# A planner that prices the first half with measured times, a second accumulation bank for the first heads, and a margin on TensorE's operands

## The chip, the cores and the metric

The kernel runs on one core of one Trainium2 chip. The metric is the device time of one execution in microseconds (us), taken as the median of several runs. TensorE is called PE in the profile's rows, its weight loads PEld, VectorE DVE, ScalarE ACT, GpSimd POOL, and SyncE's DMA queue SP.

## The reference

Three layers follow each other: a causal attention with a bias, a dense layer with a gate, and eight experts whose weights come from a balanced gate.

```python
# attention: 4 batches, 8 heads, 576 positions, 64 wide
scores = scale * q @ k^T                    # causal
bias = -(cum[:, :, :, None] - cum[:, :, None, :]);  cum = cumsum(max(s, 0))
attn = softmax(where(causal, -1e9, scores + minimum(bias, 0)))
x = (attn @ v) as 2304 rows x 512
# first MoE (one dense expert, 512 -> 2048 -> 512)
h = x @ w_in;  x = (h * sigmoid(1.702 * h)) @ w_out
# second MoE (8 experts, 512 -> 1024 -> 512)
P = exp(x @ w_gate), 8 times normalised over rows and columns
out = sum_e P[:, e] * (relu(x @ w1[e]) @ w2[e])
```

## The kernel before

The program is written once, in the order of a planner that runs while the kernel is built. Class `Sequencer` keeps a model time for each engine (`free`), for each buffer what has touched it (`touched`), and lists of operations that are handed in but not yet placed (`held`). An operation that PE executes is placed at once. Those of the other engines are held, and `run` places them when PE's model time has reached the point at which they could start, first by rank, then by number. `cost` gives each operation its model duration; there are two sets of prices, a coarse one and a finer one that holds from the second MoE on (`fine`). So the planner's prices decide in what order the instructions of every engine stand in the program; on the chip each engine executes its list in that order.

What PE does next is chosen in the loop at the end of the first half: it asks the functions `can_vpow`, `can_flush`, `can_value`, `can_turn`, `can_score` and the first MoE's generator when their operands are settled in model time, and takes the first in this list that is ready. The steps are these:

- `scores` (written `sp` in rows): q times k for a block of queries into a bank `sp`. DVE reduces it against the mask (a custom instruction, `sm<-sp,mask`, called ISA where the order of a program is listed), ACT takes the exponential. The first 8 heads read `kf` in full 32 bit; later ones read two 32-bit-rounded parts, `one` and `two`, which ACT, DVE, POOL and a DMA prepare.
- `turn` (`tp`): PE transposes the exponentials; ACT or DVE copies them out (`pf` for the first 14 heads, `ph` and `pl` after).
- `values` (`op`): the weights times v, into one bank, tag "O", which `values` (line 856) allocates from the pool `ps_a`. `finish` then lets DVE divide (`stats<-op`, `xg<-op`), and the bank is free for the next head once that is done.
- `flush_x` (`xtp`): transposes a finished block of attention rows into `xh` and `xl`.
- the first MoE (`hp`, then `acc`): for a block of 256 rows (`j`) and a pair of 128 columns (`p`), 24 products of 128x256 into `hp` and 24 into `acc`. It needs the pair's weights `wih`, `wil`, `woh`, `wol`, which `conv` makes from 64-bit words: a load `st`, two ACT steps, a DVE step `t<-st`, a cast and a subtraction on DVE or POOL. There are 8 pairs, 4 chunks each; those of pairs 4 to 6 need memory that is only given free when the first 16 heads are nearly done (`convert`).

There are 64 half heads: `heads` alternates eight times 8 heads with 256 queries or 320 queries, in 128 units. In the program stand 192 reductions `sm<-sp`, and they are used below as marks: "the 16th reduction" stands after 16 others, in both programs behind the same score step. The marks used are the 16th (the first score of the ninth head), the 40th, the 48th and the 64th.

After the attention the first MoE does its last two blocks in a wide form (`accw`, 573 to 655 us), and the second MoE follows to the end.

Of the kernel before, what the change touches and what calls it, by code (L numbers as in the profile page):

```python
# [38 lines left out]
N_KF = 4  # L39
ADDING = 3.6  # L40
AFTER_OWN = 34
N_F = 14
NEXT_V = 11
LATE = 3000.0

LATENCY = {
# [3 lines left out]


class Op:
    __slots__ = ("engine", "call", "cost", "ready", "end", "waits", "after", "rank", "number", "nbytes", "late", "tail")


class Sequencer:
# [10 lines left out]
    def __init__(self):  # L67
        self.free = dict.fromkeys(self.ENGINES, 0.0)
        self.held = {e: [] for e in self.ENGINES}
        self.touched = {}  # L70
        self.earlier = {}
        self.rings = {}
        self.dma = self.issued = 0.0
        self.rank = 0
        self.holding = False
        self.fine = False
        self.late = 0.0
        self.count = 0
        self.outside = set()
# [13 lines left out]
    def settled(self, name, ap=None):  # L93

        t = 0.0
        for x in self.touched.get(name, ()):
            if ap is not None:
                _, cols = self.where(ap)
                if x[1][0] >= cols[1] or cols[0] >= x[1][1]:
                    continue  # L100
            if x[3].end is None:
                return float("inf")
            if x[3].engine != "PE":
                t = max(t, x[3].end + 200)
        return t

    @staticmethod
# [22 lines left out]
    def cost(self, engine, what, out, ins, sums=False):  # L130
        n = max(self.size(x) for x in [out] + ins[:2])
        psum = any(x.space == PSUM for x in ins)
        if self.fine:
            if engine == "PE":
                return self.size(out) * (4 if ins[0].dtype == F32 else 1) / 2.4 + (13 if ins[0].dtype == F32R else 2.7)
            by = any(self.size(x) == 1 for x in ins[1:]) and n > 1
            if engine == "DVE":
                quick = what in ("tensor_copy", "tensor_scalar") and not psum
                return 66 + 60 * by + n / (1.92 if quick else 0.96)
            if engine == "ACT":  # L140
                return (50 if psum else 90) + 100 * by + 93 * sums + n / 1.2
        if engine == "PE":
            n = self.size(out)
            if what == "transpose":
                return 2 * n / 2.4
            slow = ins[0].dtype == F32 or ins[0].dtype == F32R and n < 256
            return n * (4 if slow else 1) / 2.4
        if engine == "DVE":
            quick = what in ("tensor_copy", "tensor_scalar") and not psum
            return 70 + n / (1.92 if quick else 0.96)  # L150
        if engine == "ACT":
            return 90 + n / 1.2
        return 80 + n * {"memset": 0.3, "tensor_scalar": 2.7}.get(what, 2.24)


    def submit(self, engine, what, call, outs, ins, adds=False):
        op = Op()
        op.engine, op.call, op.end, op.rank, op.number = engine, call, None, self.rank, self.count
        op.ready, op.waits, op.after, op.nbytes, op.tail = 0.0, set(), [], 0, 0
        op.late = self.late + (2000 if self.fine and self.rank else 0)  # L160
        self.count += 1
        if what == "dma_start":
            op.cost = 60 if engine == "SP" else 1000
            op.nbytes = self.size(outs[0]) * outs[0].shape[0] * (2 if self.fine and outs[0].dtype == F16 else 4)
            if adds and self.fine:
                op.nbytes *= ADDING
        else:
            sums = len(outs) > 1
            op.cost = self.cost(engine, what, outs[0], ins, sums) + (190 if sums and not self.fine else 0)
            if self.fine:  # L170
                op.tail = {"DVE": 85, "ACT": 110}.get(engine, 0) + 90 * sums
        for ap, writes in [(x, False) for x in ins] + [(x, True) for x in outs]:
            name = ap.tensor.name
            if name in self.outside:
                continue
            parts, cols = self.where(ap)
            mine = self.touched.setdefault(name, [])
            for x in self.touched.get(self.earlier.get(name), ()):
                self.depend(op, x[3])
            for x in mine:  # L180
                if (writes or x[2]) and x[3] is not op and not (ap.space == DRAM and writes and x[2]):
                    if x[0][0] < parts[1] and parts[0] < x[0][1] and x[1][0] < cols[1] and cols[0] < x[1][1]:
                        self.depend(op, x[3])
            mine[:] = [
                x for x in mine
                if x[3].end is None or x[3].engine != engine or x[2] != writes or x[0] != parts or x[1] != cols
            ]
            mine.append((parts, cols, writes, op))
        if engine == "PE" or not self.holding:
            self.issue(op)  # L190
        else:
            self.held[engine].append(op)

    def depend(self, op, on):
        if on.end is None:
            op.waits.add(on)
            on.after.append(op)
        elif self.fine and on.engine == op.engine != "PE" and not on.nbytes:
            op.ready = max(op.ready, on.end + AFTER_OWN)
        elif on.engine != "PE" or op.engine != "PE":  # L200
            op.ready = max(op.ready, on.end + LATENCY.get((on.engine, op.engine), LATENCY.get(on.engine, 0)))

    def issue(self, op):
# [2 lines left out]
                self.issue(x)  # L206
        e = op.engine
        start = max(self.free[e], op.ready)
        self.free[e] = start + op.cost
        op.end = start + op.cost + op.tail  # L210
        if op.nbytes:
# [7 lines left out]
        for x in op.after:  # L219
            x.waits.discard(op)  # L220
            self.depend(x, op)
        op.after = None

    def when(self, op):

# [95 lines left out]
def kernel(  # L321
# [227 lines left out]
    begin = []  # L549
# [283 lines left out]
    def turn(i):  # L833
# [21 lines left out]
        )  # L855
        live[i] = (ph, pl, blocks, spots)

    def values(i):
        n, u = units[i]
        qb0 = extent(n)[6][0]  # L860
        v3 = v3_of[n]
        ph, pl, blocks, spots = live.pop(i)
        if u[0] == qb0:
            outs[n] = (
                ps_a.tile([128, 3, D + 1], F32, tag="O", name="op"), stats[:, 8 + n % 2 * 3:11 + n % 2 * 3]
            )
        op, den = outs[n]
        for m, (qb, rows, ke, a) in enumerate(blocks):
# [97 lines left out]
    def can_value():  # L966
# [3 lines left out]
        if n > n_fin:  # L970
            return never
        x = [live[n_v][0], live[n_v][1], *v3_of[n]]
        return max([seq.slot(ps_a, "O") if n not in outs else 0] + [seq.settled(a.tensor.name) for a in x])

    def do_value():
        nonlocal n_v
# [1017 lines left out]
    while moe1_can is not None:  # L1994
# [5 lines left out]
        more_scales()  # L2000
        seq.run()
        now = seq.free["PE"]
        times = [can_vpow(), can_flush(), can_value(), can_turn(), can_score(), moe1_can()]
        which = next((k for k, x in enumerate(times) if x <= now), None)
        if which is None:
            stuck += 1
            assert stuck < 3000
# [253 lines left out]
```

## Time and profile before

| | us |
|---|---|
| median of 3 runs | 1994.37 (1994.06 to 1995.16) |
| the profiled execution, its own time | 1995.91 |
| its span, first to last instruction | 1994.1 |
| PE busy | 1956.2 (98%) |
| DVE busy | 1427.6 (72%) |
| ACT busy | 1227.5 (62%) |
| POOL busy | 335.0 (17%) |

The page cuts the span in 40 slices and shows each engine's busy share. PE's busy time counts a matmul until its modelled end, so matmuls in a row overlap; the rate is read from start to start. The view of the windows gives, for any stretch, the busy time of each engine, the clock that TensorE was granted, and the share of time in which the DMA engines moved data. The timeline gives each instruction's start and duration, and in brackets the idle time of its engine just before it and what ended it.

### The profile page before, as it was taken

Reading aid. Unit: us, or ns where it says so; the run is one execution under the profiler, and the core shown is the slowest. Engines: PE = TensorE matmul, PEld = TensorE weight load, DVE = VectorE, ACT = ScalarE, POOL = GpSimd, SP = SyncE. Lnnn points to the kernel's source line nnn. Section 1 sums busy time; section 2 is a strip of 40 time slices with the busy share of each in tenths; the row PEclk is TensorE's granted clock in tenths of the full one; section 3 lists DMA queues with packets and bytes.
Section 4 is the critical chain, followed back from the end, with each engine's and each line's share of the span. In section 5 each row is a group of like instructions: output and inputs, shape, how many; then the busy total and the mean of one; then the engine's idle time right before and its main releaser. Section 6 shows DMA issues by size and latency. Waiting matters only on the chain.

```text
span 1994.1 us, 41095 instructions
## 1 busy us (share of the span) xinstructions
PE 1956.2 (98%) x15683; PEld 1575.5 (79%) x15683; DVE 1427.6 (72%) x3240; ACT 1227.5 (62%) x2525; POOL 335.0 (17%) x376
## 2 busy tenths in 40 slices
PE   6999999999999999999999999999999999999999
PEld 5889999999988677777777777777777777777777
DVE  5886776776743776887877767776787776776656
ACT  4776765766643665665666666656666666565343
POOL 3565444443300000000000011111100001111000
PEclk9999999999999999999999999999999999999999
DMA  7555444454335544565484565666648556566331
GB/s 221 159 178 181 138 131 138 129 146 116 86 94 186 208 152 146 202 232 182 147 273 133 153 186 156 172 197 184 167 120 261 147 150 186 156 172 183 119 130 43
DMA packets 230100, 322.11 MB, mean 162 GB/s; under 512 B 38272, under 2 KB 156224, under 8 KB 229904
## 3 DMA queue, kind: packets, MB, share of 16 engines
q1 hardware_dynamic: 216944, 295.90, 45.2%
q0 software_dynamic: 12960, 23.60, 8.2%
q8 instruction: 123, 2.02, 0.4%
q14 instruction: 73, 0.60, 0.1%
HBM read 230.85 MB, written 84.34 MB: 158 GB/s over the span
## 4 chain that ended last, share of the span: by engine, by line
PE 81%; DVE 9%; ACT 6%; DMA 2%; issue 1%; SPq 0%; POOL 0%; ACTq 0%; DVEq 0%
PE C L279 16%; PE A L279 16%; PE D L279 16%; PE hp L279 8%; PE B L279 8%; PE acc L279 5%; PE op L279 3%; PE sp L279 3%; PE tp L279 2%; ACT h L279 2%; PE accw L279 2%; DVE h L279 2%; DVE t L279 1%; DVE hst L279 1%; PE accx L279 1%
## 5 line engine op out<-in xcount | busy, mean ns | idle before, releaser
L279 PEld LDWEIGHTS <-h 128*128 128x128 f16 x6048 | 591.3, 98 | 86.3 <-issue 7.6
L279 PEld LDWEIGHTS <-w1o 128*128 128x128 f16 x4036 | 394.6, 98 | 255.1 <-issue 4.5
L279 POOL DMA_DIRECT2D acc_d<-y x90 | 77.8, 865 | 1186.5 <-DVE y L279 662.1
L279 PE MATMUL C<-xt,w1o 128*128 128x384 f16 x1152 | 218.6, 326 | 1.4 <-DVE hst L279 1.4
L279 PE MATMUL D<-xt,w1o 128*128 128x384 f16 x1152 | 218.4, 326 | 0.0
L279 PE MATMUL D<-w2o,h 128*128 128x256 f16 x1728 | 217.7, 273 | 0.2 <-ACT y L279 0.2
L279 PE MATMUL A<-xt,w1o 128*128 128x384 f16 x1152 | 214.8, 326 | 0.1
L279 PE MATMUL A<-w2o,h 128*128 128x256 f16 x1728 | 212.2, 273 | 1.7 <-ACT B L279 1.4
L279 PE MATMUL C<-w2o,h 128*128 128x256 f16 x1728 | 208.4, 273 | 2.5 <-DVE y L279 1.7
L279 DVE SCALAR_TENSOR_TENSOR h<-hst,h 128x768 f16<-128x768 f32 (+1 forms) x192 | 139.1, 755 | 55.9 <-ACT h L279 55.9
L279 ACT COPY C<-B 128x384 f32<-128x384 f32 (+1 forms) x168 | 71.5, 426 | 153.8 <-PE B L279 92.7
L279 PE MATMUL hp<-xh,wih 128*128 128x256 f32 (+1 forms) x512 | 154.4, 302 | 1.3 <-DVE t L279 0.7
L279 PE MATMUL hp<-xl,wih 128*128 128x256 f32 (+1 forms) x512 | 152.0, 297 | 0.0
L279 PE MATMUL hp<-xh,wil 128*128 128x256 f32 (+1 forms) x512 | 151.8, 297 | 0.0
L279 ACT ACTIVATE h<-hst 128x768 f16<-128x768 f32 (+1 forms) x192 | 126.2, 678 | 3.8 <-DVE hst L279 3.8
L279 ACT ACTIVATE sm<-sm,stats 64x576 f32<-64x576 f32 (+4 forms) x160 | 94.5, 600 | 34.0 <-DVE stats L279 33.7
L279 PE MATMUL acc<-gh,woh 128*128 128x256 f32 x384 | 110.9, 289 | 0.0
L279 PE MATMUL B<-w2o,h 128*128 128x256 f16 x864 | 110.5, 273 | 0.1
L279 PE MATMUL B<-xt,w1o 128*128 128x384 f16 x576 | 109.3, 326 | 0.0
L279 PE MATMUL acc<-gl,woh 128*128 128x256 f32 x384 | 108.5, 282 | 0.0
L279 PE MATMUL acc<-gh,wol 128*128 128x256 f32 x384 | 108.3, 282 | 0.0
L279 ACT COPY B<-A 128x384 f32<-128x384 f32 (+1 forms) x168 | 70.2, 425 | 58.4 <-PE A L279 57.6
(242 smaller groups left out, 4041.8 us busy)
## 6 DMA issues: line engine op xcount, KB each, us to landing
xt<-xc_d SPq DMA_DIRECT2D x168, 384.0 KB
wm<-in_moe_w_dram SPq DMA_DIRECT2D x112, 256.0 KB
w2o<-w_d SPq DMA_DIRECT2D x56, 512.0 KB
wr<-in_moe_w_dram SPq DMA_DIRECT2D x112, 256.0 KB
w_d<-wo SPq DMA_DIRECT2D x98, 256.0 KB
acc_d<-y POOLq DMA_DIRECT2D x90, 256.0 KB, 4.8
kq<-in_qk_dram SPq DMA_DIRECT2D x32, 448.0 KB
st<-in_moe_w_in_dram SPq DMA_DIRECT2D x16, 512.0 KB
```

What stands on the lines that cost most here:

```text
L279: self.seq.submit(self.name, what, lambda: method(*args, **named), outs, ins, "accum_op" in named)
```

## The change

Three things. First, the finer prices of `cost`, which held from the second MoE on, hold from the start; PE gets a model of its own (`array`), in which products cost double until it has worked for `WARM` = 6300 ns without a gap, and in which a weight load counts as far as the products before it don't cover it. Second, the value step of every odd head among the first 8 allocates its bank as tag "acc0" of the pool `ps_m` (the bank that the first MoE uses later), so that two heads' values are in two banks. Third, the loop that chooses PE's next step asks first with a margin: an operand made by another engine counts as settled only `SLACK` = 1000 ns later. Only if nothing is ready with the margin does it ask without.

```diff
@@ class Sequencer: settled
             if x[3].engine != "PE":
-                t = max(t, x[3].end + 200)
+                t = max(t, x[3].end + 200 + self.slack)
@@ cost
         if engine == "PE":
...
-            return n * (4 if slow else 1) / 2.4
+            return n * (4 if slow else 1) / 2.4 + (13 if ins[0].dtype == F32R else 2.7)
+        by = any(self.size(x) == 1 for x in ins[1:]) and n > 1
         if engine == "DVE":
             quick = what in ("tensor_copy", "tensor_scalar") and not psum
-            return 70 + n / (1.92 if quick else 0.96)
+            return 66 + 60 * by + n / (1.92 if quick else 0.96)
         if engine == "ACT":
-            return 90 + n / 1.2
+            return (50 if psum else 90) + 100 * by + 93 * sums + n / 1.2
@@ submit
-            op.cost = self.cost(engine, what, outs[0], ins, sums) + (190 if sums and not self.fine else 0)
-            if self.fine:
-                op.tail = {"DVE": 85, "ACT": 110}.get(engine, 0) + 90 * sums
+            if engine == "PE":
+                op.load = 110 if BYTES[ins[0].dtype] == 4 else 27
+            op.cost = self.cost(engine, what, outs[0], ins, sums)
+            op.tail = {"DVE": 85, "ACT": 110}.get(engine, 0) + 90 * sums
@@ depend
-        elif self.fine and on.engine == op.engine != "PE" and not on.nbytes:
+        elif on.engine == op.engine != "PE" and not on.nbytes:
             op.ready = max(op.ready, on.end + AFTER_OWN)
@@ issue
+        if e == "PE" and not self.fine:
+            start = self.array(op, start)
+    def array(self, op, start):
+        idle = start > self.free["PE"] + 50
+        if idle:
+            self.since = start
+        if start - self.since > WARM:
+            self.cold = False
+        by = 2 if self.cold else 1
+        op.cost *= by
+        begin = start + max(0.0, by * op.load - (0.0 if idle else self.streamed))
+        self.streamed = op.cost
+        return begin
@@ values, can_value
+    def o_of(n):
+        return (ps_m, "acc0") if n < H and n % 2 else (ps_a, "O")
...
+            pool, tag = o_of(n)
             outs[n] = (
-                ps_a.tile([128, 3, D + 1], F32, tag="O", name="op"), stats[:, 8 + n % 2 * 3:11 + n % 2 * 3]
+                pool.tile([128, 3, D + 1], F32, tag=tag, name="op"), stats[:, 8 + n % 2 * 3:11 + n % 2 * 3]
             )
@@ the loop that chooses
-        times = [can_vpow(), can_flush(), can_value(), can_turn(), can_score(), moe1_can()]
-        which = next((k for k, x in enumerate(times) if x <= now), None)
+        for seq.slack in (SLACK, 0):
+            times = [can_vpow(), can_flush(), can_value(), can_turn(), can_score(), moe1_can()]
+            which = next((k for k, x in enumerate(times) if x <= now), None)
+            if which is not None:
+                break
+        seq.slack = 0
```

Where PE's list moves, first place: the values (`op`), transposes (`tp`) and scores (`sp`) among the later of the first 8 heads. Before:

```order
L279 MATMUL op_430<-vf0_133,pf_376 128x65 x2
L279 MATMUL op_430<-vf1_134,pf_376 128x65
L279 MATMUL tp_434<-ident_60,sm_345 128x128 x3
L279 MATMUL vtp_459<-ident_60,vmax_138 2x128
L279 MATMUL op_462<-vf0_133,pf_404 128x65 x2
L279 MATMUL op_462<-vf1_134,pf_404 128x65
L279 MATMUL tp_466<-ident_60,sm_378 128x128 x3
L279 MATMUL op_487<-vf0_133,pf_438 128x65 x2
L279 MATMUL op_487<-vf1_134,pf_438 128x65
L279 MATMUL vbp_491<-vd_412,ones_b_140 128x4
L279 MATMUL tp_493<-ident_60,sm_406 128x128 x3
```

and in the changed program:

```order
L294 MATMUL tp_463<-ident_60,sm_409 128x128 x3
L294 MATMUL op_476<-vf0_133,pf_452 128x65 x2
L294 MATMUL op_476<-vf1_134,pf_452 128x65
L294 MATMUL op_485<-vf0_133,pf_467 128x65 x2
L294 MATMUL op_485<-vf1_134,pf_467 128x65
L294 MATMUL vtp_498<-ident_60,vmax_138 2x128
L294 MATMUL xtp_513<-ident_60,xg_313 128x128 x4
L294 MATMUL xtp_521<-ident_60,xg_313 128x128 x4
L294 MATMUL vbp_538<-vd_415,ones_b_140 128x4
L294 MATMUL sp_549<-one0_112 128x384
L294 MATMUL sp_549<-two0_113 128x384
```

Two value steps now stand back to back in two banks; the pair `vtp`, `vbp` (the scale of later heads) has moved behind the eighth head, and all eight transposes `xtp` of the first rows have moved ahead of the first score of the ninth head.

Second place: PE's list between the 40th and the 48th reduction, from the end of one head to the next (`hp` is the first MoE). Before:

```order
L279 MATMUL sp<-one_112 64x288
L279 MATMUL sp<-two_113 64x288
L279 MATMUL vtp<-ident,vmax 8x128
L279 MATMUL op<-vf_133,pf 64x65
L279 MATMUL op<-vf_134,pf 64x65
L279 MATMUL op<-vf_135,pf 64x65
L279 MATMUL op<-vf_136,pf 64x65
L279 MATMUL op<-vf_137,pf 64x65
L279 MATMUL hp<-xh,wih_84 128x256
L279 MATMUL hp<-xl,wih_84 128x256
L279 MATMUL hp<-xh,wil_85 128x256
```

and in the changed program:

```order
L294 MATMUL sp<-one_112 64x288
L294 MATMUL sp<-two_113 64x288
L294 MATMUL vbp<-vd,ones_b 128x16
L294 MATMUL op<-vf_133,pf 64x65
L294 MATMUL op<-vf_134,pf 64x65
L294 MATMUL op<-vf_135,pf 64x65
L294 MATMUL op<-vf_136,pf 64x65
L294 MATMUL op<-vf_137,pf 64x65
L294 MATMUL sp<-one_114 128x384
L294 MATMUL sp<-two_115 128x384
L294 MATMUL tp<-ident,sm 128x128 x4
```

The next head's score follows where products of the first MoE stood; these have moved to an earlier place. Between the 16th and the 40th reduction's score PE's list holds 108 of them before and 168 in the changed program; between the 40th and the 48th 48 before and none now; between the 40th and the 64th 384 before and 288 now.

## Rows read from the trace of the kernel before

**Rows 1.** The page's first part: busy time, share and instructions of each engine.

```profile
PE 1956.2 (98%) x15683; PEld 1575.5 (79%) x15683; DVE 1427.6 (72%) x3240; ACT 1227.5 (62%) x2525; POOL 335.0 (17%) x376
```

**Rows 2.** Windows cut at the marks: length, busy time by engine, granted clock, DMA.

```profile
core 0: us, PE busy (x) PEld busy (x) DVE busy (x) ACT busy (x) POOL busy (x), PEclk, DMA share, GB/s
8.67:44.37 35.70, 28.43 (x105) 23.02 (x105) 23.45 (x85) 17.04 (x36) 9.67 (x8) 1.00 0.80 248
44.37:91.34 46.97, 44.94 (x357) 41.31 (x357) 40.26 (x109) 38.66 (x66) 26.55 (x26) 1.00 0.52 164
...
170.95:573.00 402.05, 398.30 (x3910) 381.75 (x3909) 282.46 (x840) 259.34 (x528) 167.18 (x185) 1.00 0.45 129
573.00:1994.00 1421.00, 1410.83 (x10646) 1060.07 (x10645) 1010.63 (x2034) 852.99 (x1777) 77.81 (x90) 1.00 0.56 168
```

**Rows 3.** PE's timeline in the first eight heads: start, duration, instruction, idle before.

```profile
17.55 2.90 PE L279 MATMUL sp<-kf 66*128 66x128 f32 x8 [0.33 <-DMA kf<-in_qk_dram]
20.38 1.51 PE L279 MATMUL op<-vf,pf 128*128 128x65 f32 x6
21.68 0.84 PE L279 MATMUL tp<-ident,sm 128*128 128x128 f32 x3
22.32 1.49 PE L279 MATMUL sp<-kf 66*128 66x128 f32 x4
24.60 1.51 PE L279 MATMUL op<-vf,pf 128*128 128x65 f32 x6 [0.79 <-DVE xg L279]
...
32.76 0.37 PE L279 MATMUL vtp<-ident,vmax 128*2 128x128 f32 x1 [1.78 <-DVE vmax L279]
...
36.24 1.51 PE L279 MATMUL op<-vf,pf 128*128 128x65 f32 x6 [1.13 <-DVE xg L279]
37.69 0.58 PE L279 MATMUL vbp<-vd,ones_b 2*128 2x4 f32 x2
...
41.54 1.52 PE L279 MATMUL op<-vf,pf 128*128 128x65 f32 x6 [2.44 <-DVE xg L279]
...
49.49 0.78 PE L279 MATMUL op<-vf,pf 128*128 128x65 f32 x6
```

**Rows 4.** The same timeline around 114 us, and one product stream at full rate.

```profile
114.75 1.09 PE L279 MATMUL xtp<-ident,xg 128*128 128x128 f32 x4
115.49 0.56 PE L279 MATMUL sp<-one 128*128 128x256 f32 x1
...
117.75 0.41 PE L279 MATMUL hp<-xh,wih 128*128 128x256 f32 x1
117.97 0.41 PE L279 MATMUL hp<-xl,wih 128*128 128x256 f32 x1
...
121.02 0.28 PE L279 MATMUL hp<-xl,wih 128*128 128x256 f32 x1
121.13 0.28 PE L279 MATMUL hp<-xh,wil 128*128 128x256 f32 x1
```

**Rows 5.** Windows of the stretch from the 40th to the 64th reduction and its last part.

```profile
91.34:170.95 79.61, 73.65 (x670) 69.33 (x669) 68.67 (x171) 57.98 (x118) 48.99 (x47) 0.96 0.54 174
107.07:170.95 63.88, 57.92 (x517) 54.84 (x516) 57.35 (x130) 48.20 (x101) 41.69 (x38) 0.95 0.59 192
...
140.00:160.00 20.00, 18.79 (x169) 18.23 (x170) 18.98 (x43) 13.81 (x28) 13.81 (x12) 1.00 0.48 152
```

**Rows 6.** DVE's `t<-st` and casts `gh`: count, duration min/median/max in ns.

```profile
L279 DVE SCALAR_TENSOR_TENSOR t<-st x32: 670/692/1796, 22.0 to 163.1; 128x512 int32<-128x512 int32 x32
...
L279 DVE CAST gh<-t x9: 414/417/428, 133.6 to 624.3; 128x512 fp32r<-128x512 f32 x9
```

**Rows 7.** Its group from 91.34 to 170.95 us: busy us, mean ns, idle before.

```profile
L279 DVE SCALAR_TENSOR_TENSOR t<-st 128x512 int32<-128x512 int32 x17 | 17.2, 1017 | 0.4 <-ACT va L279 0.3
```

**Rows 8.** Timeline of DVE and of POOL where both work, about 59 us.

```profile
59.03 1.77 DVE L279 SCALAR_TENSOR_TENSOR t<-st 128x512 int32<-128x512 int32 x1 [0.68 <-POOL wol L279]
...
57.28 2.97 POOL L279 TENSOR_TENSOR wol<-t,woh 128x512 fp32r<-128x512 f32 x2
```

More of the change, by code (lines that the diff above doesn't have):

```diff
@@ L41 @@
 AFTER_OWN = 34
+WARM = 6300
 N_F = 14
 NEXT_V = 11
+SLACK = 1000
 LATE = 3000.0
@@ L52 @@
 class Op:
-    __slots__ = ("engine", "call", "cost", "ready", "end", "waits", "after", "rank", "number", "nbytes", "late", "tail")
+    __slots__ = ("engine", "call", "cost", "ready", "end", "waits", "after", "rank", "number", "nbytes", "late", "tail", "load")
 class Sequencer:
@@ L76, in __init__ @@
         self.fine = False
+        self.slack = 0
+        self.cold, self.since, self.streamed = True, 0.0, 0.0
         self.late = 0.0
@@ L135, in cost @@
                 return self.size(out) * (4 if ins[0].dtype == F32 else 1) / 2.4 + (13 if ins[0].dtype == F32R else 2.7)
[L136 to L141, printed above, removed]
         if engine == "PE":
@@ L144, in cost @@
             if what == "transpose":
[L145 removed]
+                return 2 * n / 2.4 + 3
             slow = ins[0].dtype == F32 or ins[0].dtype == F32R and n < 256
[L147 removed]
+            return n * (4 if slow else 1) / 2.4 + (13 if ins[0].dtype == F32R else 2.7)
+        by = any(self.size(x) == 1 for x in ins[1:]) and n > 1
         if engine == "DVE":
             quick = what in ("tensor_copy", "tensor_scalar") and not psum
[L150 removed]
+            return 66 + 60 * by + n / (1.92 if quick else 0.96)
         if engine == "ACT":
[L152 removed]
+            return (50 if psum else 90) + 100 * by + 93 * sums + n / 1.2
         return 80 + n * {"memset": 0.3, "tensor_scalar": 2.7}.get(what, 2.24)
@@ L158, in submit @@
         op.engine, op.call, op.end, op.rank, op.number = engine, call, None, self.rank, self.count
-        op.ready, op.waits, op.after, op.nbytes, op.tail = 0.0, set(), [], 0, 0
+        op.ready, op.waits, op.after, op.nbytes, op.tail, op.load = 0.0, set(), [], 0, 0, 0
         op.late = self.late + (2000 if self.fine and self.rank else 0)
@@ L972, in can_value @@
         x = [live[n_v][0], live[n_v][1], *v3_of[n]]
-        return max([seq.slot(ps_a, "O") if n not in outs else 0] + [seq.settled(a.tensor.name) for a in x])
+        return max([seq.slot(*o_of(n)) if n not in outs else 0] + [seq.settled(a.tensor.name) for a in x])
     def do_value():
```

## The prediction

> **What bounds the kernel now.** I read the page's first part first: PE is busy for 1956 of 1994 us [rows 1]. Its share says little here, since it counts matmuls that overlap, so I cut the span at the marks and read the windows [rows 2, 5]. From 573 us on PE works without pause (1410.8 of 1421 us). PE's list is the same in both programs from the last products of the first MoE's narrow form on, so that stretch is worth nothing to this change. From 171 to 573 us PE is without work for only 3.75 us, with DVE at 282 of 402 us. What can be won lies before 171 us.
>
> There are two different places there. In the first heads (8.67 to 44.37 us) PE waits: it has 28.4 us of work in 35.7, and the timeline shows for what. A value step `op` waits for `xg`, DVE's division of the head before, because there is one bank: 0.79, 1.13 and 2.44 us before three of them, and 1.78 us before `vtp` [rows 3]. PE is also slow there: six `op` products take 1.30 us from start to start, four score products half of 2.90 us. From 49.49 us on six `op` take 0.78 us instead of 1.51, so these are the two levels of 1.2 and 2.4 GHz, although the column of the granted clock shows 1.00 in this window [rows 2, 3]. Where the column does show the lower level, a product `hp` takes 0.21 us from start to start; at the higher one it takes 0.12 [rows 4]. From the 40th to the 64th reduction (91.34 to 170.95 us) the picture is another: DVE is busy for 68.67 of 79.61 us, in the last 63.88 us of it for 57.35 (0.90), in the 20 us from 140 us on for 18.98 [rows 5]. There DVE sets the pace, and PE's gaps are what is left over.
>
> **Part 1, the first heads.** With the second bank and the new order no `op` follows a division of the head just before. Per head PE then issues six `op` (1.30 us), three `tp` (0.64, from 21.68 to 22.32) and four `sp` (1.45): 3.39 us at the low level, 27.1 us for eight [rows 3]. From 8.67 us, with the 0.33 us wait for a load that stays, the eighth head ends at 36.1. `vtp` 0.2, `vbp` 0.5, eight `xtp` at 0.74 per four from start to start at the low level [rows 3, 4] and the ninth head's first score with its reduction 1.1 bring 39.4. DVE's list up to that mark is 1.8 us longer by its rows' means than before, so 25.3 us of work after 10.45 us: it could be there at 35.7, which is near enough to cost PE some waits, and with the DMA engines at 0.80 [rows 2] a late load would cost the same. I take 0.6 for them: the mark at 40.0 instead of 44.37. Ahead of it now stand also the eighth head's values and eight `xtp`, 2.2 us where they stood before. **Gain 6.6 us.** Ends: if DVE's waits stay as long as now (6.9 us in the rows quoted and their like) 2.5; if PE reaches the high level about 8 us after its last gap, as it did after 41.54 us [rows 3], the heads' second half halves and DVE's 35.7 us decides: 10.
>
> **Part 2, 16th to 40th reduction.** PE gets 60 more products of the first MoE (168 for 108), 7.2 us at 0.12, and loses the 2.2 us that went ahead. At the old pace that is 46.97 + 7.2 - 2.2 = 52.0 us. In the old time lie 2.0 us without work and about 5 us at the low level, so 2.6 lost. With the margin and a run of 24 `hp` right after the score I take half of both: 49.7 us, **gain 2.3**, ends 0 and 4.6.
>
> **Part 3, 40th to 64th reduction.** The products that were done early are missing here: 288 for 384, 11.5 us less for PE, which then has at most 73.65 - 11.5 = 62.2 us of work. DVE's list is as long as before (75.7 against 76.9 us by its rows' means, not counting overlap), so 68.67 x 0.984 = 67.6 us. No PE order makes that shorter. At the old share of 0.90 it takes 75.2 us, at the best share seen, 18.98 of 20, 71.3. I take the middle, 73.3, because PE waits for DVE more often than it does now, not less. Against the old pace without the 96 products, 79.61 - 11.5 = 68.1, that is **5.2 us lost**: the early products filled gaps that now stay open, and between the 40th and the 48th reduction no first-MoE product is left. Ends 3.2 and 7.1. What is queued behind DVE here are the weights of pairs 4 to 6, whose loads SP issues as DVE frees their buffers.
>
> A price that I left as it is: `t<-st`, which makes the weights, takes 670 to 1796 ns [rows 6], 1017 on average here, 17.2 us in all [rows 7], against 0.67 alone. The long ones stand where POOL runs: 1.77 us at 59.03 us beside `wol` on POOL [rows 8]. The planner's new price for it, by the formula in the change, is 66 + 512/0.96 = 599 ns, the same with and without POOL. The Trainium skill, "SBUF — State Buffer", section "SBUF: two separate sides", says that DVE, in an operation with two SBUF inputs, and GpSimd share a port pair that is an exclusive lock, held for the whole instruction. By that rule a fixed price cannot be right; the trace agrees with it at 59 us, and the third rival below takes the rule at its worst.
>
> **Part 4, the rest.** From the 64th reduction to 573 us 3.75 us of waits can shrink by the margin; new ones can come. I take 1.5, ends 3.75 and -2. PE is the bound there, and its work is the same in sum. After 573 us: 0. The work off PE moves between ACT and DVE (casts `gh`, ACT to DVE), hidden by DVE's 30% of free time from 171 us on; without that cover each costs DVE 0.42 us [rows 6]. The added model `array` and the margin themselves issue nothing.
>
> **Sum.** 6.6 + 2.3 - 5.2 + 1.5 = 5.2 us. The profiled execution took 1995.91 us, 1.5 above the median; against it the sum is 1990.7, against the median of 1994.37 **1989.2 us**. A measurement of this kernel can tell about 0.2%, 4 us, from no change, so the forecast is faster by little more than that.
>
> **The rivals.**
>
> First, DVE does not hold PE back in part 3: if the margin lets PE work its 62.2 us through and the conversions slip later, where DVE has room, part 3 gains 5.9 instead of losing 5.2, 16.3 in all: 1978.1. For it: DVE's work needs not be done by the 64th reduction for the scores alone. Against: the lists are in fixed order, and those conversions stand before these reductions.
>
> Second, no difference: the bank was not what the first heads waited for. DVE is busy for 23.45 us there and gets 1.8 more; if every `xg` wait is only replaced by one for `pf` or `vmax`, part 1 gives its lower end of 2.5 and the sum 1.1: 1993.3. For it: `vtp` waits for `vmax`, not for a bank. Against: three of the four quoted waits name `xg`.
>
> Third, slower: DVE's conversions collide with POOL's subtractions more often, as both are pushed together between the 48th and the 64th reduction. The 16 `t<-st` there at 1.8 us instead of 1.02 add 12.5 us to a DVE that is the bound: 2001.7. It decides from a mean of 1.35 us on, where 16 x 0.33 us eat the 5.2 us. For it: rows 6 and 8, and a planner that prices no collision. Against: POOL's own share in the stretch, 48.99 of 79.61 us, hardly moves.
>
> **How the numbers follow.** The forecast with its ends, from 4 to 12 us gained, gets 0.50, the first rival 0.10: faster 0.60. The second, with all mixtures that end within 4 us, gets 0.29. The third, or a loss by low clock in the gaps of part 3, where each fall costs about 3 us as at 114 us [rows 4], gets 0.11. The ends added one way give 10 + 4.6 - 3.2 + 3.75 = 15.2 us gained, the other way 2.5 + 0 - 7.1 - 2 = 6.6 lost; they will not all fall together, and half of the first rival and most of the third may stay outside. The range is 1979 to 1997.
>
> **What would show it.** Right: no wait of `op` for `xg` longer than 0.3 us in the first heads, and the 16th reduction near 40 us; the 40th near 90; from there to the 64th some 73 us with DVE above 0.9 and PE with about 10 us of gaps, named DVE; the wide form beginning near 568 us and lasting as long as now. The forecast is wrong if the 16th reduction stands after 42 us, if PE has few gaps between the 40th and 64th, or if `t<-st` there takes over 1.3 us on average.

## The result and the profile after

| | before | after |
|---|---|---|
| median, us | 1994.21 (4 runs, 1993.97 to 1995.16) | 2013.26 (4 runs, 2012.09 to 2018.81) |
| the profiled execution, its own time | 1995.91 | 2012.09 |
| span | 1994.1 | 2010.1 |

The changed kernel takes 1.0098 times as long (95% interval 1.0081 to 1.0116): 19 us slower, where 5 us faster was forecast. The page's first part of the changed kernel, to hold against [rows 1]:

```profile
PE 1963.2 (98%) x15683; PEld 1579.2 (79%) x15683; DVE 1437.6 (72%) x3261; ACT 1214.9 (60%) x2504; POOL 333.0 (17%) x376
```

The shares say little. The windows at the same marks (the 16th, 40th, 64th and 184th reduction, the wide form; columns as in [rows 2]) do:

```profile
core 0: us, PE busy (x) PEld busy (x) DVE busy (x) ACT busy (x) POOL busy (x), PEclk, DMA share, GB/s
8.67:44.58 35.91, 30.47 (x119) 26.52 (x120) 26.75 (x91) 18.50 (x38) 9.73 (x7) 1.00 0.78 240
44.58:97.15 52.57, 50.55 (x403) 46.38 (x401) 43.68 (x109) 35.91 (x60) 34.19 (x30) 1.00 0.50 160
97.15:172.77 75.62, 63.55 (x564) 58.68 (x565) 64.77 (x175) 52.33 (x105) 41.38 (x43) 0.93 0.58 177
172.77:546.24 373.47, 364.43 (x3544) 346.51 (x3543) 264.39 (x783) 232.45 (x479) 157.96 (x179) 1.00 0.46 132
172.77:589.30 416.53, 407.49 (x3953) 387.08 (x3952) 292.95 (x866) 255.52 (x532) 165.07 (x186) 1.00 0.44 127
589.30:2010.00 1420.70, 1411.17 (x10648) 1060.51 (x10647) 1007.34 (x2023) 851.20 (x1769) 77.80 (x90) 1.00 0.56 167
```

The last window is as long as before [rows 2]. All of the loss lies ahead of 589 us, but a mark that comes later is not yet a loss, since PE may have done more of the first MoE by then. So I count, for each run and stretch, the **loss**: elapsed time minus PE's work in its list there. The work is priced the same way for every kernel: 0.12 us per product of 256 columns, as in [rows 4], the other forms by their columns in the same ratio and a fixed addition of 0.01 to 0.09 us, read from rows at the high level. The absolute value contains the low clock of the first heads, and a negative loss means that the prices are a little high; only differences between kernels count. Kernels with the same order up to the 64th reduction, profiled in different runs, differ from the 40th to the 64th by 0.3 to 2.4 us.

| loss, us | before | after | forecast of the difference | found |
|---|---|---|---|---|
| up to the 16th | 31.8 | 30.6 | 6.6 gained | 1.2 gained |
| 16th to 40th | 7.4 | 7.0 | 2.3 gained | 0.4 gained |
| 40th to 64th | 10.3 | 17.8 | 5.2 lost | 7.5 lost |
| 64th to 184th | -1.5 | 11.1 | 1.5 gained (to 573 us) | 12.6 lost |

From the 184th reduction to the wide form some 2 us come back, which makes 16.5, about what the profiled executions differ by (16.2). The largest miss is where almost nothing was forecast. PE's waits there, before (170.95 to 573 us) and after (172.77 to 589.30 us); the view sums them by the waiting instruction and by who released it: us in total, times, longest.

```profile
PE op L279 <- DVE xgl L279: 1.6, 2, 0.8
PE op L279 <- DVE xg L279: 1.3, 2, 0.8
PE vbp L279 <- DVE early L279: 0.6, 1, 0.6
PE sp L279 <- POOL one L279: 0.3, 1, 0.3
```

```profile
PE op L294 <- DVE xg L294: 1.6, 2, 0.9
PE xtp L294 <- DVE pl L294: 1.1, 1, 1.1
PE op L294 <- ACT sm L294: 0.8, 1, 0.8
PE xtp L294 <- DVE stats L294: 0.8, 1, 0.8
...
PE tp L294 <- ACT sm L294: 0.7, 2, 0.4
PE sp L294 <- POOL one L294: 0.7, 1, 0.7
PE op L294 <- DVE pl L294: 0.6, 1, 0.6
PE sp L294 <- DMA two<-one: 0.5, 1, 0.5
```

Four kinds of wait, 3.8 us, have become eleven, 8.1 us, for all that DVE, ACT, POOL and a DMA make for PE, although DVE is busy only 292.95 of 416.53 us. This is not one overloaded engine; it is operands that come a little late everywhere, in a kernel whose planner asked for a margin of 1 us. The listed waits have grown by 4.3 us, about a third of the 12.6; starts that are late by less than the view lists add to them, and some of it, up to 2 us, can be the count itself, which charges 0.09 us for each change to or from transposes.

In the first heads the timeline of PE shows the value steps' waits for `xg` gone, as forecast, and two others in their place:

```profile
32.32 2.79 PE L294 MATMUL op<-vf,pf 128*128 128x65 f32 x12
34.91 0.42 PE L294 MATMUL vtp<-ident,vmax 128*2 128x128 f32 x1
35.12 0.84 PE L294 MATMUL xtp<-ident,xg 128*128 128x128 f32 x3
37.70 1.33 PE L294 MATMUL xtp<-ident,xg 128*128 128x128 f32 x5 [1.73 <-DVE vw L294]
42.48 0.59 PE L294 MATMUL vbp<-vd,ones_b 2*128 2x4 f32 x2 [3.45 <-DVE xl L294]
42.99 0.69 PE L294 MATMUL sp<-one 128*128 128x384 f32 x1
```

The eight heads' values end at 34.9 us. The first of the two waits is for `xg` once more: the view names `vw`, but in the program this transpose waits for the division `xg` at 37.35 us. The second is before `vbp`, which needs `vd`, and DVE's timeline shows what stands in its list around that:

```profile
36.24 1.09 DVE L294 TENSOR_TENSOR one<-kq,one 64x320 fp32r<-64x320 f32 x1
37.35 0.29 DVE L294 SCALAR_TENSOR_TENSOR xg<-op,stats 128x128 f32<-128x128 f32 x1
...
37.68 1.40 DVE L294 CAST one<-kq 128x896 fp32r<-128x896 f32 x1
39.00 1.57 DVE L294 TENSOR_SCALAR vd<-ident,vw 2x2 f32<-2x2 f32 x2
40.61 0.49 DVE L294 TENSOR_TENSOR one<-kq,one 64x320 fp32r<-64x320 f32 x1
41.13 0.69 DVE L294 SCALAR_TENSOR_TENSOR t<-st 128x512 int32<-128x512 int32 x1
41.73 0.68 DVE L294 TENSOR_TENSOR xl<-xtp,xh 128x512 fp32r<-128x512 f32 x1
...
44.58 0.54 DVE L294 CUSTOM_DVE_ANT_0 sm<-sp,mask 128x384 f32<-128x384 f32 x1
```

`vd` is done at 40.57 us. What ends the wait is `xl` at 41.73, as the view says: `vtp`, `xtp` and `vbp` take turns in two banks (tag "T"), and `vbp` gets the bank of the first `xtp`, which is free only when DVE has made `xl` of it. So about half of the 3.45 us comes from the new order, which put `xtp` ahead of `vbp`. From 35.15 us until the 16th reduction at 44.58 DVE pauses only once, for 0.35 us.

### The profile page after: what moved, and what is told of

Same layout as the page of the kernel before. It is cut to its first block, busy times and chain, and to the rows that moved or that the text cites. A ratio compares the mean times of both kernels' runs of the same rounds, so it can differ in the third digit from the quotient of the medians.

```text
span 2010.1 us, 41075 instructions
## 1 busy us (share of the span) xinstructions
PE 1963.2 (98%) x15683; PEld 1579.2 (79%) x15683; DVE 1437.6 (72%) x3261; ACT 1214.9 (60%) x2504; POOL 333.0 (17%) x376
## 4 chain that ended last, share of the span: by engine, by line
PE 70%; DVE 7%; ACT 5%; issue 1%; DMA 1%; SPq 0%; POOL 0%; ACTq 0%; DVEq 0%; POOLq 0%
PE C L294 16%; PE A L294 16%; PE D L294 16%; PE B L294 8%; PE hp L294 5%; PE acc L294 3%; ACT h L294 2%; PE accw L294 2%; DVE h L294 2%; DVE hst L294 1%; PE sp L294 1%; PE tp L294 1%; PE op L294 1%; DVE sa L294 1%; DVE sb L294 1%
```

## The experiments

Three theories at first. **M**: the margin spends the first MoE's products early, and later none are left to fill waits. **P**: the measured prices put the lists of DVE and ACT in a bad order. **B**: the second bank itself costs. The table holds all eighteen runs; "planner" is the time that the planner itself counts from the 64th to the 184th reduction while it writes the program (the chip's is 348.0 us before, 373.5 after).

| run | median, us | ratio to before, 95% interval | loss to 64th | 64th to 184th | planner |
|---|---|---|---|---|---|
| before | 1994.2 | | 49.5 | -1.5 | 292 |
| after | 2013.3 | 1.0098, 1.0081 to 1.0116 | 55.4 | 11.1 | 350 |
| p_bank | 2000.6 | 1.0031, 1.0019 to 1.0043 | 53.4 | -1.0 | 298 |
| p_margin | 2003.3 | 1.0044, 1.0029 to 1.0059 | 54.5 | 3.1 | 307 |
| p_prices | 2019.6 | 1.0130, 1.0113 to 1.0146 | 56.9 | 14.9 | 344 |
| p_bank_prices | 2013.2 | 1.0095, 1.0080 to 1.0110 | 47.7 | 17.3 | 341 |
| q_pe_old | 2002.7 | 1.0044, 1.0029 to 1.0059 | 54.8 | -1.0 | 296 |
| q_off_old | 2018.6 | 1.0121, 1.0106 to 1.0136 | 49.4 | 18.6 | 346 |
| q_jit190 | 2005.8 | 1.0052, 1.0035 to 1.0069 | 54.3 | 0.2 | 294 |
| q_jit230 | 1999.2 | 1.0022, 1.0013 to 1.0032 | 48.2 | 0.2 | 296 |
| r_switch | 1993.9 | 0.9996, 0.9987 to 1.0006 | 46.6 | -2.9 | 295 |
| r_pe13 | 2012.6 | 1.0092, 1.0077 to 1.0107 | 50.2 | 13.2 | 335 |
| r_array | 2010.9 | 1.0081, 1.0066 to 1.0096 | 51.0 | 13.3 | 312 |
| r_off115 | 2007.7 | 1.0065, 1.0050 to 1.0080 | 44.2 | 14.1 | 344 |
| s_after_switch | 2005.6 | 1.0056, 1.0042 to 1.0070 | 56.0 | 1.1 | 308 |
| s_iso | 1991.2 | 0.9989, 0.9980 to 0.9998 | 46.6 | -4.9 | 328 |
| s_pe4 | 1994.6 | 0.9999, 0.9990 to 1.0008 | 49.1 | -2.7 | 306 |
| s_best | 1994.5 | 1.0005, 0.9996 to 1.0014 | 45.2 | 2.3 | 299 |
| t_iso_margin | 1996.4 | 1.0010, 1.0001 to 1.0020 | 47.6 | -5.1 | 330 |
| t_iso_array | 2005.8 | 1.0058, 1.0043 to 1.0073 | 52.0 | 3.6 | 345 |

### One part of the change at a time

The kernel before with `o_of` alone (p_bank), with the margin alone (p_margin), with the prices and `array` alone (p_prices); and the changed kernel without its margin (p_bank_prices):

```diff
-SLACK = 1000
+SLACK = 0
```

> The kernel before with the second bank alone. The changed kernel has lost about 19 us (2013.3 against 1994.2): 5.3 us less gain than forecast up to the 16th reduction, and 10 to 12 us between the 64th reduction and the end of the first half, where PE waits for products of DVE and ACT. Theory M (the margin spends the first MoE's products early, so that later nothing is left to fill the waits for DVE): bank alone 1988 to 1993, the waits of the first heads for xg go, nothing else changes much. Theory P (the measured prices make the planner lay out the lists of DVE and ACT wrongly): the same 1988 to 1993. Theory B (the second bank itself costs, since it moves vtp and vbp ahead of the ninth head's score): over 2000.

> The kernel before with the margin of 1000 ns alone, at the coarse prices and with one bank. Theory M: 2005 to 2015, and between the 64th and the 184th reduction some 10 us of PE waits for DVE and ACT as in the changed kernel. Theory P: within 4 us of 1994. Theory B: within 4 us of 1994.

> The kernel before with the measured prices and PE's own model alone, one bank, margin 0. Theory M: within 4 us of 1994. Theory P: 2005 to 2015, with the waits for DVE and ACT after the 64th reduction. Theory B: within 4 us of 1994.

> The changed kernel with the margin at 0: bank and measured prices. Theory M: 1988 to 1994, the loss is gone. Theory P: 2005 to 2015, the loss stays. Theory B: above 2000, with the wait before vbp near 42 us still there.

Measured: each part alone is slower, by 6.5, 9.1 and 25.4 us (medians in the table). The prices cost most, as theory P had it, and theirs is the one large loss after the 64th reduction: 14.9 and 17.3 us, against -1.0 for the bank and 3.1 for the margin. Theory B's wait before `vbp` is there (3.5 us in p_bank_prices), but not from the second bank: p_prices, with one bank, has 2.4 us of it too, and p_bank none. The margin on top of bank and prices is worth nothing in the sum (2013.3 against 2013.2): it takes 7.7 us up to the 64th and gives 6.2 back after it. PE's waits after the 64th in p_bank_prices:

```profile
PE hp L294 <- DVE t L294: 4.4, 4, 2.0
PE op L294 <- DVE pl L294: 3.4, 8, 0.9
PE sp L294 <- DVE stats L294: 2.3, 5, 1.1
PE tp L294 <- DVE xl L294: 2.2, 3, 0.9
PE op L294 <- DVE xg L294: 1.0, 2, 0.5
PE sp L294 <- DMA two<-one: 0.9, 1, 0.9
```

p_bank also settles the first heads. Its PE is ready with the ninth head's first score near 40 us, as forecast:

```profile
39.23 1.33 PE L279 MATMUL xtp<-ident,xg 128*128 128x128 f32 x5 [1.66 <-DVE xg L279]
40.21 0.67 PE L279 MATMUL sp<-one 128*128 128x384 f32 x1
...
44.60 0.58 PE L279 MATMUL hp<-xl,wih 128*128 128x256 f32 x1 [2.02 <-DVE xl L279]
```

and its 16th reduction still stands at 44.47, because DVE's list has the weights and `xl` ahead of it:

```profile
40.57 1.36 DVE L279 SCALAR_TENSOR_TENSOR t<-st 128x512 int32<-128x512 int32 x1
...
43.87 0.68 DVE L279 TENSOR_TENSOR xl<-xtp,xh 128x512 fp32r<-128x512 f32 x1
44.47 0.54 DVE L279 CUSTOM_DVE_ANT_0 sm<-sp,mask 128x384 f32<-128x384 f32 x1
```

### Which price

The measured prices have two sides. q_pe_old takes TensorE's back (and `array`, as shown here), q_off_old those of DVE and ACT; both keep the second bank and have the margin at 0:

```diff
...
-            return n * (4 if slow else 1) / 2.4 + (13 if ins[0].dtype == F32R else 2.7)
+            return n * (4 if slow else 1) / 2.4
...
-        if e == "PE" and not self.fine:
-            start = self.array(op, start)
```

q_jit190 and q_jit230 change `end + 200` in `settled` to 190 and 230, in the kernel before.

> The changed kernel with margin 0 and TensorE at its coarse price (256 columns 106.7 ns, no array), while DVE and ACT keep the measured prices and the bank stays. Theory C (the planner's TensorE was too fast per product, 106.7 ns where the chip needs 120, so the chip gave every operand of another engine some 10% more time than the planner had counted; the measured price takes that away): 1990 to 1998, with under 3 us of PE waits from the 64th reduction to the wide form, as in the kernel before (3.7) and not as with all measured prices (17.1). Theory O (the measured prices of DVE and ACT, which know no collision with POOL, put their lists in a bad order): above 2007, with over 10 us of waits there. Theory J (the order of the kernel before is a lucky draw, any other costs 5 to 10 us): 1999 to 2005.

> The counterpart: margin 0, TensorE at the measured price with its model, DVE and ACT at the coarse prices, bank in. Theory C: above 2005, with over 8 us of PE waits from the 64th reduction to the wide form. Theory O: 1990 to 1998 with under 4 us there. Theory J: 1999 to 2005.

> The kernel before with one number changed that means nothing on the chip: an operand counts as settled 190 ns after its end in the planner, not 200. It measures what a mere other order costs. Theory J: 1999 to 2005. Theories C and O: within 4 us of 1994.2.

> The same with 230 ns for 200. Theory J: 1999 to 2005. Theories C and O: within 4 us of 1994.2.

Measured after the 64th: -1.0 with TensorE coarse, 18.6 with TensorE measured. Theory C holds for this stretch, theory O falls. But q_pe_old as a whole is 8 us slower than before, with 54.8 lost by the 64th, outside theory C's 1990 to 1998, so theory J has a part too: a number that means nothing to the chip costs 4 and 11 us. The 6.5 us of the bank alone and the 9.1 of the margin alone are no larger than that, so neither is shown to cost by itself. For 190, 6.5 us of that are there at the 184th reduction; the rest comes later, since this number holds in the second MoE as well. What is learnt from the total of a single run of this planner is uncertain by 4 to 11 us; the loss after the 64th reduction, in which the two stand at 0.2, tells more.

### The cause by itself

r_switch keeps p_bank_prices up to the 64th reduction, then prices TensorE coarsely; s_after_switch does the same to the changed kernel with its margin:

```diff
...
         if engine == "PE":
             n = self.size(out)
+            if self.reductions >= 64:
+                slow = ins[0].dtype == F32 or ins[0].dtype == F32R and n < 256
+                return n * (2 if what == "transpose" else 4 if slow else 1) / 2.4
...
-        if e == "PE" and not self.fine:
+        if e == "PE" and not self.fine and self.reductions < 64:
```

> Bank and measured prices, margin 0, as in the run of 2013.2 us; but from the 64th reduction on TensorE is priced coarsely again (DVE and ACT stay measured). The order is that run's up to the 64th reduction. Theory C (TensorE's measured price takes away the time that operands of other engines had): the first 64 reductions as there, the 64th at 163 to 164 us; from there to the 184th elapsed time minus TensorE's work within -2 to +3 us instead of +17.3, and the whole 1993 to 1999. Theory O (DVE's and ACT's measured prices): no change after the 64th, 2010 to 2016. Theory J (any new order costs 5 to 10, wherever it lies): 2000 to 2012.

> The changed kernel as it is, with bank, margin and measured prices, but from the 64th reduction on TensorE is priced coarsely. Theory C: the order and the time up to the 64th as in the changed kernel (172.8 us, loss 55.4), from there to the 184th a loss of 0 to 3 us instead of 11.0, the whole 2001 to 2006. If the margin is what costs time after the 64th: no change, 2010 to 2015.

Measured: 17.3 becomes -2.9, and 11.1 becomes 1.1, with the same order up to the switch. Nothing else differs, so the loss after the 64th is shown to be TensorE's price (with its `array`), in the changed kernel too. A mere other order doesn't explain it: of the kernels in the table, the nine with TensorE's coarse price after the 64th lose between -2.9 and 3.1 us there, the six with the whole 13 ns and unscaled latencies between 11.1 and 18.6. Of PE's waits listed above, r_switch has these left:

```profile
PE tp L299 <- DVE xl L299: 0.9, 1, 0.9
PE op L299 <- DVE xg L299: 0.4, 1, 0.4
PE sp L299 <- DVE stats L299: 0.4, 1, 0.4
PE op L299 <- DVE xgl L299: 0.2, 1, 0.2
```

The windows from the 64th to the 184th reduction, of p_bank_prices and of r_switch:

```profile
163.40:536.60 373.20, 355.86 (x3456) 335.77 (x3455) 257.02 (x776) 228.06 (x461) 156.72 (x177) 1.00 0.44 128
```

```profile
162.30:513.60 351.30, 348.95 (x3440) 333.74 (x3440) 261.25 (x768) 228.18 (x457) 154.83 (x176) 1.00 0.47 136
```

About the same work of every engine, in 22 us less; 17.3 us of PE without work have become 2.4.

How much time an operand has can be read as well. In the program each instruction of PE names those of DVE and ACT that it waits for; the trace has the end of the last of them and the start of PE's. From the 64th to the 184th reduction there are some 300 such pairs. In p_bank_prices PE starts 1.17 us after its operand is done (the median), and in 57 of 286 pairs less than 0.3 us after; in r_switch it is 1.56 us, and 14 of 291. Over all twenty kernels the seven that lose 11 us or more there have 35 to 57 such close pairs (the changed kernel 47), the other thirteen 7 to 27 (the kernel before 11). The margin does lengthen the median, from 1.58 us before to 2.46 in p_margin, but in the changed kernel it is 1.58 again.

### Dose and ratio

r_pe13 adds to the kernel before only the 13 ns per product, r_array only `array`, s_pe4 a third of the 13 ns. r_off115 takes p_bank_prices with DVE, ACT and POOL 1.15 dearer. s_iso takes r_pe13 and multiplies every other duration of the first half by 1.13: steps off PE, latencies, the 200 ns, loads (parts of its edit):

```diff
+            return n * (4 if slow else 1) / 2.4 + (13 if ins[0].dtype == F32R else 2.7)
...
+            if engine != "PE" and not self.fine:
+                op.cost *= 1.13
...
-                t = max(t, x[3].end + 200)
+                t = max(t, x[3].end + 200 * self.far())
...
-            self.dma = max(self.dma, self.issued + 1200) + op.nbytes / 360
+            self.dma = max(self.dma, self.issued + 1200 * self.far()) + self.far() * op.nbytes / 360
```

> The kernel before with one part of TensorE's measured price alone: 13 ns more per 32-bit-rounded product, 2.7 per other, 3 per transpose; no model of cold clock and weight loads, DVE and ACT coarse, one bank, margin 0. Theory C: from the 64th to the 184th reduction a loss of 8 us or more, and the whole above 2005. If the loss comes from the other part (weight loads and cold clock): that loss under 3 us, the whole 1996 to 2005.

> The other part alone: cold clock and weight loads by array, with the products at the coarse price; DVE and ACT coarse, one bank, margin 0. Theory C: the planner's TensorE is then between the two (from the 64th to the 184th reduction it counts 312 us, against 292 before and 335 with the 13 ns), so the loss there should lie between, 2 to 8 us. If the loss comes from this part: over 10 us there and the whole above 2008.

> Bank and measured prices, margin 0, but each price of DVE, ACT and POOL in the first half times 1.15, TensorE measured. Theory C in its strict form (it is the ratio of the others' prices to TensorE's that counts): a loss of under 5 us from the 64th to the 184th reduction instead of 17.3, and the whole 1994 to 2003. If the order of DVE's and ACT's lists or the absolute prices decide: over 10 us there, above 2008.

> The kernel before with the 13 ns per product (2012.6 us alone), and every other duration of the planner in the first half times 1.13: steps of DVE, ACT, POOL, latencies, the 200 ns, loads. If it is the ratio of TensorE's price to all the rest that counts, the loss from the 64th to the 184th reduction is under 4 us instead of 13.2, as in the kernel before (-1.5), and the whole 1993 to 2006. If a measured TensorE price hurts by itself: over 9 us there, above 2006.

> A third of the dose: 4 ns per product, 0.8 per other, 1 per transpose, everything else as in the kernel before. The planner then counts 306 us from the 64th to the 184th reduction (292 before, 335 with 13 ns). If the loss grows with the price: 2 to 6 us there. If it jumps at a small step, as the run with the model of weight loads suggests (312 us, 13.3 lost): over 9 us. If it needs the full price: under 1.

Measured after the 64th: r_pe13 13.2, r_array 13.3, s_pe4 -2.7, so a third of the dose costs nothing, and `array` alone costs as much as the 13 ns. The loss does not simply follow the planner's count (-2.7 at 306 us, 13.3 at 312); whether it is a step, two doses of one kind and one of another don't show. s_iso loses -4.9: with the same TensorE price as r_pe13, 18 us less. **So a right price of TensorE does no harm by itself; it does harm when the rest is not raised with it.** That is near to what must be: a planner whose times are all multiplied by one number writes the same order, and divided by its 1.13 the planner's count of s_iso is 290, next to 292 before (its order is another, with 324 products of the first MoE from the 40th to the 64th reduction for 384). s_iso is not a planner with right prices, but one with the reserve put back. r_off115 contradicts the simple form, in which the prices of the steps are enough (344/1.15 is 299, and it still loses 14.1). It leaves latencies and loads unscaled and has the model of weight loads in. As a whole s_iso is the one kernel here that is faster than before, by 3 us, with an interval that just leaves out 1. It is the best of twenty orders, and an order by itself is worth 4 to 11 us, so this is no proof that its prices are better than those before; it is 22 us faster than the changed kernel.

### The margin again, and a candidate

t_iso_margin puts the margin of 1000 ns on s_iso, t_iso_array puts `array` on it. s_best joins the start of r_off115 (44.2 lost at the 64th) to the end of r_switch.

> The margin of 1000 ns on top of the kernel in which every duration of the first half is 1.13 times the coarse one and TensorE has the 13 ns (1991.2 us, 46.6 lost at the 64th reduction, -4.9 from there to the 184th). If the margin costs before the 64th by itself (it takes products of the first MoE early, and from the 40th to the 64th none is left to fill PE's waits for DVE): 51 to 55 lost at the 64th, 0 to 3 after it, the whole 1996 to 2003. If the margin cost only together with the wrong ratio: within 4 us of 1991.

> The model of weight loads and of the cold clock on top of the same kernel. It makes the planner's TensorE 5.4% dearer again from the 64th to the 184th reduction (345 us for 327), in ratio to the rest the same as in the run with 4 ns per product, which lost nothing there. If only the ratio counts: a loss of -3 to +3 us there, the whole 1990 to 2000. If this model hurts by where it puts the steps after transposes and narrow products: 8 us or more there, the whole above 2000.

> A candidate: bank, measured prices, margin 0; up to the 64th reduction the prices of DVE, ACT and POOL times 1.15 (that run had the smallest loss at the 64th, 44.2 against 49.5 us in the kernel before), from there on DVE and ACT at the measured prices and TensorE coarse (that run lost -2.9 from there to the 184th). If the two halves add: the 64th at 159 us, no more than 2 us lost after it, the whole 1986 to 1992. If each half depends on the other's order: 1992 to 2003.

Measured: with `array` the loss after the 64th is 3.6, the count 345/1.13 = 305. That is 8.5 more than in s_iso and 6.3 more than s_pe4 lost with 306, so the ratio of the counts is not all; and it is 10.5 less than r_off115's 14.1. The model of weight loads can be a part of r_off115's loss, not the whole; unscaled latencies and loads, or the measured prices off PE that it also had, are left, and which of them was not tried. Before the 64th `array` cost 5.4 us, about what an order costs by itself. The margin costs 1.0 us up to the 64th here and nothing up to the wide form, which both begin at 563.0 us. The 5 us between the medians come right behind that: PE waits 3.4 us for `gh` in the wide form, and the granted clock of the window 563 to 663 us is 0.97, for 1.00 in s_iso. From 563.03 us the wide form takes 93.87 us for 87.27 in s_iso, 6.6 more: the wait, and about as much again at the lower level. I take that for an accident of the order at the seam, not for the margin's aim; no run shows it. s_best misses: 2.3 us lost after the 64th and no faster than before, so the halves do not simply add.

For the stretch from the 40th to the 64th the runs can be put together by how many products of the first MoE PE's list has in it. The seven kernels with 288 to 312 lose 11.5 to 18.2 us there, 15.2 on average; the thirteen with 324 to 408 lose 7.8 to 15.3, 10.2 on average. The margin lowers that number from 384 to 312 (p_margin) and from 324 to 288 (after), and both lose some 7 us more; in t_iso_margin it raises it from 324 to 348, and nothing is lost. This fits theory M for that stretch; a run that sets this number alone was not made.

## Why the prediction was wrong

**Part 1 failed in its maximum.** "25.3 us of work after 10.45 us: it could be there at 35.7" for DVE, against PE's 39.4, with 0.6 us for waits. PE's side held: the heads' values end at 34.9 us, and in p_bank the first score starts at 40.2. But DVE had only part of its list done by then, since its work on a head waits for PE's: of the 24.70 us from 10.45 to 35.15 it is busy for 17.78. What is left, `one`, `vd`, `xl` and the weights, follows behind PE's last head, 9.4 us with one pause of 0.35. The two engines' totals stand partly in series, and I took the larger one. The lower end had the reason ("if DVE's waits stay as long as now (6.9 us in the rows quoted and their like) 2.5"): they stayed at 6.9. Gain 1.2 instead of 6.6. `vtp` and `vbp` I priced as PE's 0.2 and 0.5 us; the 3.45 us wait before `vbp` was the chain between them on DVE, with DVE's list in front, until 40.57 us, and then the bank that `xtp` held.

**Part 2** had 2.3 us and got 0.4; in p_bank and p_margin too this stretch hardly moves (7.7 and 6.9, for 7.4).

**Part 3 was near in size, and its reason fits**: 75.62 us for 73.3, 7.5 us lost for 5.2, just past its end of 7.1. The reason given, early products that are missing here, fits the twenty kernels, though no run shows it alone. That DVE sets the pace is not shown: DVE's share was 0.86, as over the whole stretch before [rows 5], and not above 0.9: the longest waits are one of 3.2 and one of 1.5 us, and the granted clock is 0.93 for 0.96.

**Part 4 failed, and with it the sum.** "From the 64th reduction to 573 us 3.75 us of waits can shrink by the margin; new ones can come. I take 1.5, ends 3.75 and -2." I looked at the margin alone, and took the new prices for a mere correction; for PE I wrote that `array` and the margin "themselves issue nothing". Shown by r_switch, s_after_switch and s_iso: the coarse price of a product, 106.7 ns by the formula where the chip needs 120 [rows 4], was the reserve. The planner wanted a step's operand at a point that the chip's PE reached some 12% later, so everything made off PE had that much more time. With PE priced right and the rest still priced short, that time is gone (close pairs: 57 in p_bank_prices for 14 in r_switch), and operands are late, 0.3 to 2 us at a time. In place of a gain of 1.5 us stands a loss of 12.6.

What is priced short can be read in the profile, though no run changes it alone. DVE's groups from 172.77 to 546.24 us of the changed kernel (count, then busy us and mean ns):

```profile
L294 DVE SCALAR_TENSOR_TENSOR t<-t,hp 128x512 f32<-128x512 f32 x42 | 28.6, 681 | 31.3 <-ACT t L294 31.3
L294 DVE SCALAR_TENSOR_TENSOR wb<-wa,early,wb 128x256 f16<-128x256 f32 x48 | 26.1, 562 | 10.2 <-ACT wb L294 7.9 <-DMA wa<-in_moe_w_dram 2.1
L294 DVE SCALAR_TENSOR_TENSOR pl<-tp,ph 128x384 f16<-128x384 f32 x39 | 21.3, 547 | 2.4 <-ACT ph L294 2.3
L294 DVE TENSOR_TENSOR xb<-xa,xb 128x192 f16<-128x192 f32 x35 | 17.7, 525 | 2.0 <-ACT xb L294 2.0
L294 DVE TENSOR_TENSOR wa<-wa 128x256 f32<-128x256 f32 x16 | 11.1, 694 | 0.3
```

The price and its tail of 85 ns make 684 for `t<-t,hp` and 551 for `pl`, as measured: their `hp` and `tp` lie in PSUM. For those with both inputs in SBUF they make 478 for `wb`, 351 for `xb` and 418 for `wa`, and the chip needs 562, 525 and 694; over these counts 48 x 0.084 + 35 x 0.174 + 16 x 0.276 = 14.5 us that the planner doesn't know of. The Trainium skill, "SBUF — State Buffer", section "SBUF: two separate sides", has a reason for this split: DVE with two SBUF inputs and GpSimd lock a shared port pair from each other. The trace agrees. Where no POOL instruction runs during them, `wb` takes 478 ns, `xb` 347 and `wa` 418, as priced; beside one, 713, 712 and 969. `t<-t,hp` takes 682 and 679, `pl` 547 and 547. Nor is it only instructions with two SBUF inputs: the cast `gh<-t` takes 416 alone and 608 beside POOL.

**The rivals.** The first (PE works through part 3) did not happen, and the second came true for part 1. The third named the right side and the wrong place: `t<-st` from the 40th to the 64th was not longer but shorter, 937 ns for 1017 [rows 7], far from the 1.35 us at which it decides:

```profile
L294 DVE SCALAR_TENSOR_TENSOR t<-st 128x512 int32<-128x512 int32 x16 | 14.9, 937 | 0.9 <-ACT st L294 0.6 <-POOL wil L294 0.3
```

Its sentence that a fixed price cannot be right was the lead; I applied it to one instruction in one stretch, and not to the planner's balance in all of them. The range (1979 to 1997) had no case in which a better price makes a worse order.

## What to carry to other kernels

In a program whose order comes from a model, prices matter in relation to the price of the engine that bounds: here an underpriced bottleneck was a hidden reserve on every operand, and whoever corrects that one price must put the reserve back, as s_iso does by scaling the rest, latencies and loads too (r_off115, which scales the steps alone, still lost). A reserve in time on one kind of question (the margin) does not replace it. And measure first what a meaningless change of the planner costs (here 4 and 11 us): improvements below that need a count by stretch, not a total.

## What was not expected of the hardware

An instruction's length need not lie in its elements. The two `vd` of 2x2 elements took 1.57 us from 39.00 us on, beside a subtraction `two` on POOL (39.16 to 40.56), and 0.62 us in p_bank at 35.05, where `wil` ran on POOL until 35.52. Read one by one, one of the two takes 0.21 us in both, and the other lasts until POOL's step is done: from 39.13 to 40.58 us here, from 35.06 to 35.55 in p_bank, and from 36.03 to 36.71 in the kernel before, beside a `two` that ends at 36.69. What differs is when POOL's step ends.

What a late operand costs can be more than the wait: the 3.4 us of waiting for `gh` in t_iso_margin stand beside a granted clock of 0.97 over 100 us, a wide form that is 6.6 us longer, and 5 us in the median.
